# Moving the last pair's two GpSimd sums to VectorE in a spectral-mixing and SiLU kernel

## The chip, the cores and the metric

The kernel runs on one core of one Trainium2 chip. A core has five engines with separate instruction streams: TensorE (PE, matmuls, with its weight loads shown as PEld), VectorE (DVE), ScalarE (ACT), GpSimd (POOL) and SyncE (SP, which here only issues DMA). They wait for each other through semaphores. The metric is device time in microseconds (us), lower is better. The span that a profile shows is from the first to the last instruction of one execution; the time reported for that execution is a little longer.

## The reference

Two blocks follow each other. The first is a circular convolution over the sequence, by FFT; the second is a two-layer network with SiLU on every token.

```python
def _attn_ref(x, filt_r, filt_i):          # x: (8, 3008, 256)
    X = np.fft.rfft(x, axis=1)
    F = (filt_r + 1j * filt_i)[None, :, :]
    y = np.fft.irfft(X * F, n=x.shape[1], axis=1)
    return y.astype(np.float32)

def _moe_ref(x, w_in, w_out):              # x: (24064, 256), w_in: (256, 2048), w_out: (2048, 256)
    h = x @ w_in
    g = h * (1.0 / (1.0 + np.exp(-h)))
    return (g @ w_out).astype(np.float32)
```

## The kernel before

The transforms are done as small matrix products and spread over the kernel as hidden work; their pieces are put at fixed places of a timetable. The frame of the kernel is the second block. The tokens are cut into 48 pairs of token groups (256 or 240 tokens to a group); each pair goes through 8 steps, one for two blocks of 128 of the 2048 hidden channels. A step has two halves: `hidden(step)` makes the hidden values (seven products instead of eight, after Strassen, with the sums that this needs on VectorE and ScalarE, and SiLU on ScalarE), and `project(step)`, one step later, multiplies them with the second weight and accumulates seven products in four PSUM banks, `acc` 0 to 3. Both halves are generators, taken in turn, so that the order of the instructions on each engine is written out by hand. No scheduler changes it.

When the eighth step of a pair has been accumulated, the sums in PSUM become four output blocks. For all pairs but the last this is done by `drain` (from line 1093 on): ScalarE and VectorE copy the banks into a tile `s` of 8 slots in SBUF, GpSimd makes seven sums of slots, and SyncE issues two stores. The last pair has nothing behind it that could hide this, so it has its own function, `drain_last` (line 1107, called at line 1086 of `project`), which takes each half bank as soon as its last product is there. `(i, h)` names bank and half. The slots are filled in this order: copies on ScalarE for 0, 4 and 1 (line 1114), sums on VectorE, which read one operand from PSUM, for 2, 5, 3 and 6, and at last slot 1 from slots 3 and 1. Slot 4, the sum of slots 4, 1 and 5, needs two sums of slots that lie in SBUF. Slots 2, 6, 1 and 4 are the outputs; `store` (line 1143) sends each one with a DMA of its own, on SyncE's queue (2 and 6) or ScalarE's (4 and 1).

All sums go through the helper `combine`, so they carry line 989 on whichever engine they run. After the last instruction of the kernel body each engine runs a closing sequence (line 1517): it drains, SyncE waits for all outstanding stores, every engine reports to GpSimd by a semaphore, and GpSimd then releases the engines and clears the semaphores.

Of the kernel before, what the change touches and what calls it, by code (L numbers as in the profile page):

```python
# [49 lines left out]
ALU = mybir.AluOpType  # L50
# [197 lines left out]
def kernel(  # L248
# [9 lines left out]
    nc = tc.nc  # L258
# [726 lines left out]
    v, gp = nc.vector, nc.gpsimd  # L985
    ty, g_t, acc, unfinished = {}, {}, {}, []

    def combine(eng, out, in0, in1, op):
        eng.tensor_tensor(out=out, in0=in0, in1=in1, op=op)  # L989
# [74 lines left out]
    def project(step):  # L1064

        pair, jp = divmod(step, NJP)
        n, g = pairs[pair][3], g_t.pop(step)
        if jp == 0:
            acc[pair] = {}
        last = jp == NJP - 1  # L1070

        order = PROJECT
        if jp == 0 and step in joined:
            order = PROJECT[0:2] + PROJECT[3:5] + PROJECT[2:3] + PROJECT[5:]
        elif jp == 0:
            order = PROJECT[2:3] + PROJECT[0:2] + PROJECT[3:]
        elif step == n_steps - 1:
            order = PROJECT[0:4] + PROJECT[5:6] + PROJECT[4:5] + PROJECT[6:]
        for c, k, i, h in order:
            if i not in acc[pair]:  # L1080
                acc[pair][i] = accps.tile([128, 2, 256], FP32, name=f"acc_{pair}_{i}", tag=f"a{i}")

            nc.tensor.matmul(out=acc[pair][i][:, h, 0:n], lhsT=w_t[:, jp, c, 1], rhs=g[:, k, 0:n],  # L1083
                             start=(jp == 0 and h == 0), stop=last, skip_group_check=True)
            if last and pair == len(pairs) - 1:
                drain_last(pair, i, h, n, acc[pair])
            elif last and (h == 1 or i == 3):
                drain(pair, i)
            yield
# [17 lines left out]
    def drain_last(pair, i, h, n, sums):  # L1107

        if pair not in results:
            results[pair] = spool.tile([128, 8, CH], FP32, name=f"s_{pair}", tag="s")  # L1110
        s = results[pair]

        def copied(slot):
            nc.scalar.copy(out=s[:, slot, 0:n], in_=sums[i][:, h, 0:n])  # L1114

        def add(o, a, b=None, eng=v):
            combine(eng, s[:, o, 0:n], s[:, a, 0:n], sums[i][:, h, 0:n] if b is None else s[:, b, 0:n], ALU.add)
        if (i, h) == (0, 0):
            copied(0)
        elif (i, h) == (1, 0):  # L1120
            add(2, 0)
            store(pair, 2, nc.sync)
        elif (i, h) == (2, 0):
            copied(4)
        elif (i, h) == (0, 1):
            copied(1)
            add(4, 4, 1, gp)
        elif (i, h) == (2, 1):
            add(5, 0)
            add(4, 4, 5, gp)  # L1130
            store(pair, 4, nc.scalar)
        elif (i, h) == (1, 1):
            add(3, 5)
        else:
            add(6, 3)
            store(pair, 6, nc.sync)
            add(1, 3, 1)
            store(pair, 1, nc.scalar)

    def store(pair, slot, queue):  # L1140

        n = pairs[pair][3]
        queue.dma_start(out=out[pair, OUT_SLOTS.index(slot), :, 0:n], in_=results[pair][:, slot, 0:n])
# [378 lines left out]
```

## Time and profile before

| what | value |
|---|---|
| time, median of 3 runs | 2532.5 us (2532.28 to 2534.07) |
| time of the profiled execution | 2532.73 us |
| its span | 2530.6 us |
| granted TensorE clock | 0.996 |
| TensorE busy | 2505.6 us, 99% |
| VectorE, ScalarE, GpSimd busy | 69%, 43%, 17% |

On the page, a group's row gives the line, the engine and the operation, the output and the input tile, the partitions and elements, and the count; then the busy time and the mean length of one. A row of the timeline gives start and length in us from the start of the span, and in brackets the engine's idle time ahead of it with what released it. Rows of instructions that an engine's sequencer handles by itself (drains, semaphores, DMA issues) have a q behind the engine's name, and are not counted as busy.

### The profile page before, as it was taken

What the parts mean: (1) busy time and instruction counts of PE and PEld (TensorE: products, weight loads), DVE (VectorE), ACT (ScalarE), POOL (GpSimd) and SP (SyncE); (2) the same over time, 40 slices, a digit from 0 to 9 for tenths busy, and PEclk for the clock granted to TensorE, in tenths of its full rate; (3) what the DMA queues carried; (4) which work ended last, traced back from release to release, by engine and by line L of the source; (5) the groups of instructions that cost most, each with busy time, mean ns of one, the idle gap of its engine ahead of it and who ended that gap; (6) DMA issues with size and microseconds to landing.
All of it is one profiled execution on the core that took longest, in us unless ns stands there. A gap on an engine that the chain in (4) does not pass through costs nothing. (4 is left out here: it accounts for less than half of the span.)

```text
span 2530.6 us, 42130 instructions
## 1 busy us (share of the span) xinstructions
PE 2505.6 (99%) x16122; PEld 2142.8 (85%) x16122; DVE 1750.1 (69%) x3619; ACT 1096.7 (43%) x3012; POOL 435.1 (17%) x681
## 2 busy tenths in 40 slices
PE   8999999999999999999999999999999999999998
PEld 6788888888888888888888888888888888888987
DVE  7866777777767777677776767767677667655544
ACT  2544444444444444444444444444444444444443
POOL 3211211022111121211221112211121111101101
PEclk9999999999999999999999999999999999999999
DMA  9622142312332132420324203331142211200000
GB/s 289 169 67 88 63 109 58 80 51 63 76 85 63 41 80 59 95 73 20 92 58 108 60 25 77 85 72 43 28 107 58 55 43 34 63 21 9 17 9 17
DMA packets 145218, 171.49 MB, mean 68 GB/s; under 512 B 21396, under 2 KB 118772, under 8 KB 144132
## 3 DMA queue, kind: packets, MB, share of 16 engines
q1 hardware_dynamic: 119752, 117.85, 18.0%
q0 software_dynamic: 22272, 45.68, 7.0%
q10 hardware_dynamic: 2992, 5.28, 0.7%
q8 instruction: 126, 2.06, 0.4%
q14 instruction: 76, 0.62, 0.1%
HBM read 96.88 MB, written 81.26 MB: 70 GB/s over the span
## 5 line engine op out<-in xcount | busy, mean ns | idle before, releaser
L1083 PE MATMUL acc<-g,w_t 128*128 128x256 f32 (+1 forms) x5376 | 1509.5, 376 | 4.2 <-DVE q L818 3.7
L1083 PEld LDWEIGHTS acc<-g,w_t 128*128 128x128 f32 x5376 | 1017.1, 190 | 150.5 <-DVE q L818 19.0
L989 DVE TENSOR_TENSOR g<-pyz,abc 128x256 f32<-128x256 f32 (+1 forms) x1152 | 479.3, 416 | 501.7 <-ACT abc L1039 259.9
L989 DVE TENSOR_TENSOR g<-g 128x256 f32<-128x256 f32 (+3 forms) x1152 | 589.8, 512 | 196.9 <-ACT g L1022 183.7
L1018 PE MATMUL px<-ty,w_t 128*128 128x256 f32 (+1 forms) x2304 | 679.3, 377 | 1.5 <-ACT abc L1033 0.6
L1022 ACT ACTIVATE g<-g 128x256 f32<-128x256 f32 (+1 forms) x1152 | 472.9, 410 | 243.0 <-DVE g L989 243.0
L989 POOL TENSOR_TENSOR s<-s 128x256 f32<-128x256 f32 (+1 forms) x331 | 253.3, 783 | 1504.1 <-DVE s L1101 1099.8
L1018 PEld LDWEIGHTS px<-ty,w_t 128*128 128x128 f32 x2304 | 433.0, 190 | 65.3 <-ACT abc L1033 6.9
L1018 PE MATMUL pyz<-y,w_t 128*128 128x256 f32 (+1 forms) x1536 | 453.2, 377 | 0.8 <-DVE g L989 0.6
L1018 PEld LDWEIGHTS pyz<-y,w_t 128*128 128x128 f32 x1536 | 283.6, 190 | 46.4 <-DVE g L989 6.3
L1033 ACT COPY abc<-px 128x256 f32<-128x256 f32 (+1 forms) x384 | 141.4, 368 | 367.4 <-PE px L1018 367.4
L1039 ACT COPY abc<-px 128x256 f32<-128x256 f32 (+1 forms) x384 | 141.8, 369 | 312.9 <-PE px L1018 312.8
L1022 ACT ACTIVATE g<-px 128x256 f32<-128x256 f32 (+1 forms) x384 | 146.1, 381 | 302.0 <-PE px L1018 302.0
L1018 PE MATMUL px<-y,w_t 128*128 128x256 f32 (+1 forms) x768 | 228.0, 379 | 0.9 <-DVE y L775 0.9
L1018 PE MATMUL pyz<-ty,w_t 128*128 128x256 f32 (+1 forms) x768 | 226.0, 376 | 0.2 <-DVE g L989 0.2
L1018 PEld LDWEIGHTS px<-y,w_t 128*128 128x128 f32 x768 | 144.1, 190 | 26.1 <-ACT t L447 4.9
L1018 PEld LDWEIGHTS pyz<-ty,w_t 128*128 128x128 f32 x768 | 142.2, 190 | 21.4 <-DVE g L989 1.0
L1026 ACT COPY abc<-px 128x256 f32<-128x256 f32 (+1 forms) x384 | 135.5, 353 | 37.2 <-PE px L1018 37.2
L1101 ACT COPY s<-acc 128x512 f32<-128x512 f32 (+1 forms) x94 | 54.3, 578 | 47.5 <-issue 28.5
L646 POOL DMA_DIRECT2D d<-low x36 | 22.3, 618 | 288.9 <-DVE low L642 288.9
L818 DVE STREAM_TRANSPOSE q<-pd 128x512 f32<-128x512 f32 x84 | 57.2, 699 | 3.2 <-PE pd L797 3.2
L827 DVE TENSOR_TENSOR y<-q 128x384 f32<-128x384 f32 x112 | 56.1, 542 | 0.0
(159 smaller groups left out, 1367.5 us busy)
## 6 DMA issues: line engine op xcount, KB each, us to landing
t<-d SPq DMA_DIRECT2D x84, 256.0 KB
t<-d SPq DMA_DIRECT2D x224, 96.0 KB
out_dram<-s SPq DMA_DIRECT2D x64, 256.0 KB
d<-q POOLq DMA_DIRECT2D x48, 256.0 KB, 5.3
d<-low POOLq DMA_DIRECT2D x36, 256.0 KB, 4.2
xr<-in_x_dram SPq DMA_DIRECT2D x6, 1472.0 KB
out_dram<-s SPq DMA_DIRECT2D x30, 240.0 KB
x_all<-in_x_dram SPq DMA_DIRECT2D x72, 96.0 KB
```

Of the source, the lines that this page charges most:

```text
L646: nc.gpsimd.dma_start(out=d2[a0:a0 + 8, 16 * end:16 * end + 16], in_=part)
L818: nc.vector.transpose(out=t.rearrange("p (n a c) -> p n a c", n=8, a=2), in_=us["pd", k][r].rearrange("p a c -> p (a c)").rearrange("p (n ...
L827: nc.vector.tensor_tensor(out=dst[:, :, :, at:at + n], in0=even[:, :, :, 0:n], in1=odd[:, :, :, 0:n], op=op)
L989: eng.tensor_tensor(out=out, in0=in0, in1=in1, op=op)
L1018: nc.tensor.matmul(out=out, lhsT=w_t[:, jp, c, 0], rhs=rhs, start=start, stop=True, skip_group_check=True)
L1022: nc.scalar.activation(out=g[:, k, 0:n], in_=g[:, k, 0:n] if src is None else src, func=AFT.Silu)
L1026: nc.scalar.copy(out=sums[:, 0, 0:n], in_=xo)
L1033: nc.scalar.copy(out=sums[:, 1, 0:n], in_=xo)
L1039: nc.scalar.copy(out=sums[:, 2, 0:n], in_=xo)
L1083: nc.tensor.matmul(out=acc[pair][i][:, h, 0:n], lhsT=w_t[:, jp, c, 1], rhs=g[:, k, 0:n], start=(jp == 0 and h == 0), stop=last, skip_group ...
L1101: copy(out=s[:, 2 * i:2 * i + 2, 0:n], in_=acc[pair][i][:, :, 0:n])
```

## The change

For the last pair, slot 4's two sums move from GpSimd to VectorE. The first (slots 4 and 1) moves from the place of bank 0, half 1 to that of bank 2, half 1, behind VectorE's sum of slot 5. The second (slots 4 and 5) and slot 4's store move from there to the place of bank 1, half 1, behind VectorE's sum of slot 3. The store stays on ScalarE's queue. GpSimd's last sum is then the seventh one of `drain` for the pair before.

```diff
-        def add(o, a, b=None, eng=v):
-            combine(eng, s[:, o, 0:n], s[:, a, 0:n], sums[i][:, h, 0:n] if b is None else s[:, b, 0:n], ALU.add)
+        def add(o, a, b=None):
+            combine(v, s[:, o, 0:n], s[:, a, 0:n], sums[i][:, h, 0:n] if b is None else s[:, b, 0:n], ALU.add)
...
         elif (i, h) == (0, 1):
             copied(1)
-            add(4, 4, 1, gp)
         elif (i, h) == (2, 1):
             add(5, 0)
-            add(4, 4, 5, gp)
-            store(pair, 4, nc.scalar)
+            add(4, 4, 1)
         elif (i, h) == (1, 1):
             add(3, 5)
+            add(4, 4, 5)
+            store(pair, 4, nc.scalar)
         else:
             add(6, 3)
             store(pair, 6, nc.sync)
```

On each engine the order of all other instructions stays the same.

## The prediction

> **What bounds the kernel now.** I read the page first, then the chain of waits near the end, then the stretches of the last microseconds, and last the closing instructions one by one, since only the tail is edited.
>
> ```profile
> span 2530.6 us, 42130 instructions
> ...
> PE 2505.6 (99%) x16122; PEld 2142.8 (85%) x16122; DVE 1750.1 (69%) x3619; ACT 1096.7 (43%) x3012; POOL 435.1 (17%) x681
> ```
>
> TensorE is busy for 99% of the span. Nothing in the diff touches a matmul, so the first 2522 us stay as they are; both kernels issue the same instructions in the same order on TensorE, ScalarE and SyncE, and on VectorE and GpSimd they differ only behind the last matmuls. What can move is the stretch after TensorE. The chain of waits there, as start, length and work:
>
> ```profile
> 2522.49 0.69 PE acc L1083 x2
> 2523.17 0.02 issue
> 2523.20 0.42 DVE s L989
> ...
> 2523.71 0.40 DVE s L989
> 2524.11 0.32 DVEq L1517
> ```
>
> The chain stops at 2524.11 + 0.32 = 2524.43, but the span runs to 2530.6. The last 6.2 us are on no row of the chain. The busy time by stretch says the same:
>
> ```profile
> 2522.50:2524.20 1.70, 1.06 (x4) 0.66 (x4) 1.30 (x4) 0.00 (x0) 1.38 (x2) 1.00 0.21 72
> 2524.20:2530.60 6.40, 0.00 (x0) 0.00 (x0) 0.23 (x1) 0.00 (x0) 0.00 (x0) 0.63 0.17 59
> ```
>
> Columns: stretch, length, then PE, PEld, DVE, ACT, POOL busy (times), clock, DMA share, GB/s. In the last 6.4 us only the end of one VectorE operation and some DMA are left. So the closing sequence (line 1517, issued by the program's end) must hold the time. Its rows, from four windows: engine and operation, count, ns min/median/max, first and last start.
>
> ```profile
> L1517 PEldq DRAIN  x1: 1120/1120/1120, 2522.5 to 2522.5; - x1
> L1517 POOLq DRAIN  x1: 6534/6534/6534, 2523.3 to 2523.3; - x1
> L1517 DVEq DRAIN  x1: 699/699/699, 2523.8 to 2523.8; - x1
> ...
> L1517 SPq EVENT_SEMAPHORE  x2: 28/28/28, 2526.1 to 2526.4; - x2
> L1517 SPq DRAIN  x2: 7/7/7, 2526.5 to 2526.5; - x2
> ...
> L1517 POOLq EVENT_SEMAPHORE  x4: 17/17/17, 2529.9 to 2530.5; - x4
> L1517 POOLq DRAIN  x3: 46/102/6534, 2523.3 to 2530.3; - x3
> ```
>
> Each engine drains and then reports; SyncE first waits for the last stores (its last two such waits pass at 2526.1 and 2526.4) and reports at 2526.5. GpSimd's drain starts at 2523.3 and lasts 6.534 us, to 2523.3 + 6.53 = 2529.8. Only then does GpSimd take the reports (2529.9), and 0.7 us later the program is over. GpSimd's drain is the last to come, 2529.8 - 2526.5 = 3.3 us after SyncE. That drain, not TensorE and not the stores, sets the end.
>
> **Why the drain is so late.** GpSimd's operations in the last 50 us, as start, length, operation, count and the idle time before:
>
> ```profile
> 2479.77 5.70 POOL L989 TENSOR_TENSOR s<-s 128x256 f32<-128x256 f32 x7 [42.52 <-DVE s L1101]
> 2522.55 1.46 POOL L989 TENSOR_TENSOR s<-s 128x240 f32<-128x240 f32 x2 [37.08 <-ACT s L1114]
> ```
>
> The second row is the two sums that the change takes away. The drain is issued while the second of them begins (2523.3). That one ends at 2522.55 + 1.46 = 2524.01, so the drain ends 2529.8 - 2524.0 = 5.8 us after GpSimd's last work. VectorE's drain ends at 2523.8 + 0.70 = 2524.5, 0.1 after its last sum. The 5.8 us belong to GpSimd alone.
>
> **The change, part by part.** First: GpSimd loses two sums. Its last operation then ends at 2479.77 + 5.70 = 2485.47. The drain comes next in its stream with no wait ahead of it, so it is issued there; if it again takes 5.8 us behind the last sum, it ends near 2491.3, under TensorE's work, which covers it until 2522. It would need 35 us more to matter. The end then goes by whichever engine reports last, SyncE at 2526.5: a gain of 3.3 us.
>
> Second: VectorE gets two sums in a row of five. VectorE's closing sums before, one a row, then the ScalarE copy that the first new sum needs:
>
> ```profile
> 2522.04 0.40 DVE L989 TENSOR_TENSOR s<-s,acc 128x240 f32<-128x240 f32 x1
> 2522.51 0.40 DVE L989 TENSOR_TENSOR s<-s,acc 128x240 f32<-128x240 f32 x1
> 2523.20 0.41 DVE L989 TENSOR_TENSOR s<-s,acc 128x240 f32<-128x240 f32 x1 [0.29 <-PE acc L1083]
> 2523.71 0.40 DVE L989 TENSOR_TENSOR s<-s,acc 128x240 f32<-128x240 f32 x1
> 2524.03 0.40 DVE L989 TENSOR_TENSOR s<-s 128x240 f32<-128x240 f32 x1
> ...
> 2522.06 0.36 ACT L1114 COPY s<-acc 128x240 f32<-128x240 f32 x1 [0.79 <-PE acc L1083]
> ```
>
> They are slots 2, 5, 3, 6, 1. The last two stand 2524.03 - 2523.71 = 0.32 us apart although each lasts 0.40, so a sum that waits for nothing recent starts 0.32 us behind the one before. The first new sum (4 + 1) goes between slots 5 and 3: its inputs are copies, the last of which ended at 2522.42, so it starts at 2522.51 + 0.32 = 2522.83 and ends at 2523.23. Slot 3 waits for TensorE until 2523.20, and VectorE could take it from 2522.83 + 0.32 = 2523.15: no delay. The second new sum (4 + 5) follows at 2523.20 + 0.32 = 2523.52 and ends at 2523.92. Slot 6 stood at 2523.71 and can start only at 2523.52 + 0.32 = 2523.84: **0.13 us late**. Slot 1 follows at 2524.16 instead of 2524.03, 0.13 late as well.
>
> Bounds of this cost, from the nearest rows. It cannot be below nothing: no sum on the way to the last store gets an earlier input. Its upper end is two dependent sums back to back:
>
> ```profile
> 2515.80 0.84 DVE L989 TENSOR_TENSOR g<-g 128x240 f32<-128x240 f32 x2
> ```
>
> So 0 to 0.84 us; I take 0.13, as the row with the 0.32 spacing is from the very place.
>
> One rule speaks for more. The Trainium skill, "VectorE: DVE Perf Modes", section "The DRAIN you can't avoid", says in substance that the next VectorE operation doesn't start until the pipe of the one before is empty. By it the five sums would stand 0.40 apart: 4 + 1 until 2523.31, slot 3 from there, 4 + 5 until 2524.12, slots 6 and 1 until 2524.92, against 2524.43 before: +0.49. The overlap of the last two rows above disagrees, so I keep 0.13.
>
> Third: the stores. The issues before, and the share of the DMA engines in 40 slices from 2524.8 to 2526.8:
>
> ```profile
> 2524.04 0.36 ACTq L1143 DMA_DIRECT2D out_dram<-s  x1
> 2524.14 0.35 SPq L1143 DMA_DIRECT2D out_dram<-s  x1
> L1143 ACTq DMA_DIRECT2D out_dram<-s x2: 363/397/431, 2524.0 to 2524.5; - x2
> DMA  0037998999999999999999520000000000000000
> ```
>
> Slot 4's store on ScalarE's queue waited for GpSimd until 2524.01; now it waits for VectorE until 2523.92 and goes 0.09 us earlier. Slot 6's store on SyncE's queue and slot 1's behind slot 4's on ScalarE's go 0.13 later. Slot 4's issue ends at 2523.95 + 0.36 = 2524.31, before slot 1's sum does (2524.56), so it holds nothing up. The three stores fill the DMA engines almost without a gap until 2526.0, so the delay can pass on at most whole: SyncE's report goes from 2526.5 to 2526.6. No wait is added on TensorE: its last matmuls wait for VectorE's first sum (slot 2), which stands ahead of both new ones.
>
> **The sum.** -3.3 (drain gone from the end) + 0.13 (VectorE) = -3.2 us. Span 2530.6 - 3.2 = 2527.4. The profiled execution took 2532.73, 2.1 more than its span, so 2529.5; it lay 0.2 above the median of the runs (2532.5), so I predict **2529.4 us**, 0.12% below. A measurement of this kernel tells from no change only about 0.2% (5.1 us), so this counts as no change.
>
> **Rivals.** (a) The drain doesn't follow GpSimd's work but the end of the whole core, for example the last stores. It ended 3.4 us after SyncE's last store wait (2526.4), a distance no row explains. Then the change removes nothing and VectorE's delay of 0.13 to 0.84 is left: 2532.6 to 2533.3, slower than before from the first 0.1 us on. Against it: drains of the other engines end with their own work, and the drain at the program's start did too:
>
> ```profile
> L1506 POOLq DRAIN  x1: 174/174/174, 0.3 to 0.3; - x1
> L1506 POOL MEMSET const-uint8-127<- x1: 106/106/106, 0.3 to 0.3; 128x1 uint8 x1
> ```
>
> There the last memset is also at 0.3 and the drain lasts 0.17. It shows that a GpSimd drain can be short, but behind memsets and not behind sums. The same section of the Trainium skill calls the closing drains a constant of about 12 ns on all five engines, another kind than VectorE's; taken at its word GpSimd's own drain costs nothing, the 6.5 us would be a wait for something else, and (a) follows. The trace disagrees with the 12 ns (6,534 ns). Chance of (a) 0.08.
>
> (b) The 5.8 us fall on the first drain that GpSimd makes after standing idle, and come back in the closing sequence: GpSimd drains twice more behind the reports (46 and 102 ns above, right behind the long one), now after 35 us of waiting. At full price the end is 2527.4 + 5.8 = 2533.2, the time 2535.2; it is slower than before once more than 3.2 of the 5.8 us return. Against it: after 37.08 us of idling GpSimd's first sum lasted as long as the next (1.46 for both, with the gap). Chance 0.04.
>
> (c) The drain moves, but VectorE's sums stand serially or the stores collide, so that up to 0.84 is given back: 2530.0. It has the same sign and lies within my forecast.
>
> **How the numbers follow.** Forecast with (c): 0.86; (a) 0.08; (b) 0.04; unnamed 0.02. The forecast's bounds are 2529.2 (no VectorE delay) to 2530.0 (0.84 of it). The shown runs scatter from 0.2 below their median to 1.6 above, and the closing times are read to 0.1 us only, so I take 2528.6 to 2531.7. (a) and (b) lie outside it, 0.12 together. The bound of 0.2% is 2527.4 below and 2537.6 above: forecast, (a) and (b) all lie between. Same 0.92, faster 0.05 (a floor lower than the stores show, or run scatter), slower 0.03.
>
> **What would show it.** Right: GpSimd's long drain starts near 2485 and ends near 2491; GpSimd's first closing semaphore stands 0.1 us behind SyncE's report, near 2526.7; the span is 2527.4; five VectorE sums become seven, with slot 1's starting at 2524.16. Wrong by (a): a drain from 2485 to 2529 or later. Wrong by (b): one of the two later drains in microseconds. A last sum near 2524.5 instead of 2524.2 would show serial spacing.

## The result, and the profile after

The changed kernel takes 2528.59 us, the median of 22 runs (2526.49 to 2532.10); the kernel before, run beside it as often, takes 2532.44 us (2529.77 to 2538.01). The ratio is 0.9984, with a 95% interval of 0.9978 to 0.9989: a small gain, about 3.9 us. The prediction was 2529.4 us (range 2528.6 to 2531.7): the right direction and mechanism, the gain 0.8 us too small, so that the median lies just below the lower end of the range.

The profiled execution took 2527.65 us. The first line of the changed kernel's page:

```profile
span 2525.8 us, 42128 instructions
```

GpSimd's timeline in its last 50 us (start, length, operation, count, idle time before):

```profile
2478.39 5.71 POOL L989 TENSOR_TENSOR s<-s 128x256 f32<-128x256 f32 x7 [42.52 <-DVE s L1101]
```

And rows of its closing sequence (line 1517) from three windows, in the form used in the prediction:

```profile
L1517 POOLq DRAIN  x1: 7251/7251/7251, 2482.7 to 2482.7; - x1
...
L1517 SPq EVENT_SEMAPHORE  x10: 17/28/28, 2523.3 to 2524.9; - x10
...
L1517 POOLq EVENT_SEMAPHORE  x2: 17/17/17, 2525.1 to 2525.2; - x2
L1517 SPq DRAIN  x1: 7/7/7, 2525.1 to 2525.1; - x1
L1517 POOLq DRAIN  x1: 102/102/102, 2525.3 to 2525.3; - x1
```

GpSimd's long drain now starts at 2482.7 and ends at 2482.7 + 7.25 = 2489.9, again 5.8 us behind its last sum (2478.39 + 5.71 = 2484.10), under TensorE's work. At the end SyncE's last store wait passes at 2524.9, SyncE reports at 2525.1, and GpSimd takes the reports in the same tenth. The 3.3 us between the two are gone. VectorE's timeline of the changed kernel, its seven closing sums:

```profile
2520.65 0.87 DVE L989 TENSOR_TENSOR s<-s,acc 128x240 f32<-128x240 f32 x2
2521.44 0.40 DVE L989 TENSOR_TENSOR s<-s 128x240 f32<-128x240 f32 x1
2521.82 0.40 DVE L989 TENSOR_TENSOR s<-s,acc 128x240 f32<-128x240 f32 x1
2522.14 0.40 DVE L989 TENSOR_TENSOR s<-s 128x240 f32<-128x240 f32 x1
2522.46 0.40 DVE L989 TENSOR_TENSOR s<-s,acc 128x240 f32<-128x240 f32 x1
2522.77 0.40 DVE L989 TENSOR_TENSOR s<-s 128x240 f32<-128x240 f32 x1
```

Slots 2 and 5 share the first row; then come 4 + 1, 3, 4 + 5, 6 and 1. From slot 3 on they stand 0.32, 0.32 and 0.31 us apart though each lasts 0.40.

**Where the rest of the difference lies.** The two profiled executions differ by 5.1 us (2532.73 - 2527.65). Take two marks that both kernels have, GpSimd's sums of an early pair and of the last pair but one; the rows are from the kernel before:

```profile
198.27 5.56 POOL L989 TENSOR_TENSOR s<-s 128x256 f32<-128x256 f32 x7 [47.16 <-DVE s L1101]
```

and from the changed one:

```profile
196.83 5.57 POOL L989 TENSOR_TENSOR s<-s 128x256 f32<-128x256 f32 x7 [47.15 <-DVE s L1101]
```

The changed kernel is already 1.44 us ahead at 198 us (198.27 - 196.83), and still 1.38 ahead at 2480 (2479.77 - 2478.39). So 1.4 us arose before the first 200 us were over, where both kernels issue the same instructions, and nothing in the 2280 us between. The stretch from 50 to 100 us shows a likely source; its columns are PE, PEld, DVE, ACT, POOL busy (times), clock, DMA share, GB/s, first before, then changed:

```profile
50.00:100.00 50.00, 44.53 (x437) 33.86 (x437) 41.59 (x100) 26.31 (x56) 7.23 (x15) 0.83 0.77 227
```

```profile
50.00:100.00 50.00, 43.71 (x443) 32.10 (x442) 43.83 (x105) 26.79 (x57) 9.04 (x18) 0.90 0.76 224
```

There the granted clock was 0.83 and 0.90; over the whole first 156 us it was 0.95 and 0.96. In the twelve other profiles of this study TensorE passes the mark of 156 us between 3.7 us ahead of the kernel before and 2.9 us behind it (0.9 without the run with three drains below, which has two of them in that stretch), and keeps that distance to within 0.1 us until its end. The executions with the lower clock in the first 156 us tend to pass the mark later (0.93: 0.9 us behind; 1.00: 3.7 us ahead), but the clock isn't all of it: 0.98 stands beside 0.4 and beside 1.7 us ahead. So the 1.4 us are run scatter, and its cause is only in part shown.

That is why below the **tail** is compared: from the start of VectorE's sum of slot 3 to the end of the span. It was 2530.6 - 2523.20 = 7.4 us and is 2525.8 - 2521.82 = 4.0, a gain of 3.4. A last 0.3 us lies outside the span: the time around it fell from 2.1 (2532.73 - 2530.6) to 1.8 (2527.65 - 2525.84). The three parts, 1.4 + 3.4 + 0.3, make the 5.1.

### The profile page after: what moved, and what is told of

Its sections match the earlier page's. It is cut to its first block, busy times and chain, and to the rows that moved or that the text cites. A ratio compares the mean times of both kernels' runs of the same rounds, so it can differ in the third digit from the quotient of the medians.

```text
span 2525.8 us, 42128 instructions
## 1 busy us (share of the span) xinstructions
PE 2504.1 (99%) x16122; PEld 2140.9 (85%) x16122; DVE 1750.5 (69%) x3621; ACT 1095.2 (43%) x3012; POOL 433.7 (17%) x679
## 3 DMA queue, kind: packets, MB, share of 16 engines
q10 hardware_dynamic: 2992, 5.28, 0.7%
q8 instruction: 126, 2.06, 0.3%
```

## The experiments

All are profiled once on the chip; all but one start from the changed kernel. Tails and moments are read from the trace, counted in us from the start of VectorE's sum of slot 3 (written +/-).

**What starts the drain.** Three runs give GpSimd one operation back, whose result nobody reads.

A one-column copy, where the removed first sum stood:

```diff
             copied(1)
+            gp.tensor_copy(out=gate, in_=s[:, 1, 0:1])
```

> The changed kernel with one more GpSimd operation: a copy of one column of slot 1 into an unused tile, waiting for ScalarE's copy of slot 1, as the removed first sum did. Nothing reads it; VectorE keeps both sums. The tail is counted from the start of VectorE's slot 3 sum to the end of the span: 7.4 us before (2530.6 - 2523.20), 4.0 changed (2525.8 - 2521.82). Theory A (GpSimd's closing drain ends 5.8 us behind GpSimd's last operation of any kind): the copy starts some 0.65 us ahead of slot 3 and lasts a few tenths, the drain ends at +5.35, the tail is 6.1. Theory B (the 5.8 us come behind two-input sums only): 4.0. Theory C (the drain follows the end of the whole core): 7 or more.

A whole sum at that place:

```diff
             copied(1)
+            combine(gp, s[:, 7, 0:n], s[:, 4, 0:n], s[:, 1, 0:n], ALU.add)
```

> The changed kernel with one more GpSimd operation: the sum of slots 4 and 1 into the unused slot 7, 128x240, where the removed first sum stood. VectorE keeps both sums. It should end at about +0.04 us of slot 3's start. Theory A: drain until +5.85, tail 6.6. Theory B: the same. Theory C: no relation to the 0.04.

A memset:

```diff
             add(5, 0)
+            gp.memset(s[:, 0, 0:n], 0.0)
             add(4, 4, 1)
```

> The changed kernel with one more GpSimd operation: a memset of slot 0 (128x240) once VectorE's sum of slot 5 has read it, about 0.2 us ahead of slot 3. Theory A: it ends near 0.0 to +0.2, drain until +5.8 to +6.0, tail 6.5 to 6.8. Theory B, in the wider sense that only operations that read SBUF leave the 5.8 us (at the program's start the drain came 0.05 us behind a memset): tail 4.0.

| kernel | GpSimd's last operation ends | its drain ends | between | SyncE reports | tail |
|---|---|---|---|---|---|
| before | +0.82 | +6.62 | 5.81 | +3.34 | 7.4 |
| changed | -37.7 | -31.9 | 5.81 | +3.25 | 4.0 |
| late copy | -0.53 | +5.28 | 5.81 | +3.26 | 6.1 |
| late sum | -0.36 | +5.45 | 5.81 | +3.24 | 6.2 |
| late memset | +0.07 | +5.88 | 5.81 | +3.26 | 6.7 |

GpSimd's last operation in the run with the memset, from its timeline:

```profile
2523.30 0.30 POOL L1129 MEMSET s<- 128x240 f32 x1 [37.50 <-DVE s L989]
```

Its drain, from the rows of the closing sequence:

```profile
L1518 POOLq DRAIN  x1: 6126/6126/6126, 2523.3 to 2523.3; - x1
```

The memset ends at 2523.60 and the drain at 2523.3 + 6.13 = 2529.4: 5.8 us later, as behind a copy of one column and behind a sum. So the kind of operation doesn't matter (theory B falls), and the drain doesn't go by the stores' end (theory C, the prediction's rival (a)). The tail is the later of drain and report plus 0.8. In the run with the sum slot 3 itself starts 0.4 us late, because VectorE's 4 + 1 has to wait until GpSimd has read slot 4; counted from slot 2's sum the tail is 7.8, against 8.6 before, by the 0.8 us of the missing second sum.

**How early is early enough.** A copy released 3.9 us and one released 2.4 us ahead of slot 3's sum:

```diff
         silu(3, xo)
+        if step == n_steps - 1:
+            gp.tensor_copy(out=gate, in_=g[:, 3, 0:1])
```

> The changed kernel with a one-column GpSimd copy that waits for ScalarE's activation of slot 3 of the last step's hidden tile, which ends at 2517.88, 3.9 us ahead of VectorE's slot 3 sum. Theory A: the copy ends near -3.7, the drain near +2.1, SyncE's report (+3.25) stays the last and the tail stays 4.0. If GpSimd work anywhere in the last pair prolonged the end, the tail would be over 4.3.

```diff
             copied(0)
+            gp.tensor_copy(out=gate, in_=s[:, 0, 0:1])
```

> The changed kernel with a one-column GpSimd copy that waits for ScalarE's copy of slot 0, which ends at 2519.41, 2.4 us ahead of VectorE's slot 3 sum. Theory A: the copy ends near -2.2, the drain near +3.6, just behind SyncE's report at +3.25; the tail is 4.3 to 4.4. A drain with a shorter tail behind copies than behind sums leaves 4.0.

The first ends at -3.70, its drain at +2.11, and the tail is 4.0: free. The second ends at -1.92, its drain at +3.88, and the tail is 4.7, not the 4.3 to 4.4 expected, because this copy lasted 0.43 us where the others took 0.18 and 0.19; VectorE was adding from SBUF until just before it ended, which is the likely reason. Again 5.81 lie between, in both. So on this kernel GpSimd has to be done about 2.6 us (5.81 - 3.25) ahead of slot 3's sum, or it sets the end.

**GpSimd's part alone, undone.** Two GpSimd sums into an unused slot, with VectorE's two left in place:

```diff
             copied(1)
+            combine(gp, s[:, 7, 0:n], s[:, 0, 0:n], s[:, 1, 0:n], ALU.add)
...
             add(4, 4, 1)
+            combine(gp, s[:, 7, 0:n], s[:, 7, 0:n], s[:, 5, 0:n], ALU.add)
```

> The changed kernel with two more GpSimd sums into the unused slot 7, waiting for the same things as the two that the change removed; VectorE keeps its two. Only GpSimd's part of the change is undone. If that part alone makes the gain: drain until +6.6, tail 7.4, as before. If VectorE's two sums cost or gain something of their own, the tail differs from 7.4 by it (0.13 at most by the prediction).

The tail is 7.2, and counted from slot 2's sum 8.6 as before: all that the change gained in the tail is lost again, so it was GpSimd's part. But VectorE's sums look different while GpSimd adds at the same time. VectorE's timeline of this run, from 4 + 1 to 4 + 5:

```profile
2522.90 0.68 DVE L989 TENSOR_TENSOR s<-s 128x240 f32<-128x240 f32 x1
2523.50 0.39 DVE L989 TENSOR_TENSOR s<-s,acc 128x240 f32<-128x240 f32 x1
2523.82 0.58 DVE L989 TENSOR_TENSOR s<-s 128x240 f32<-128x240 f32 x1
```

GpSimd's timeline of the same run:

```profile
2522.62 1.50 POOL L989 TENSOR_TENSOR s<-s 128x240 f32<-128x240 f32 x2 [37.08 <-ACT s L1114]
```

The two sums with both operands in SBUF take 0.68 and 0.58 instead of 0.40; the one between, which reads one operand from PSUM, keeps its 0.39. The Trainium skill, "GPSIMD Engine Reference", section "Specifications", says that the two engines share SBUF interfaces and contend when a VectorE instruction has two SBUF inputs; this run agrees.

**VectorE and the stores.** More VectorE work, and another order of it:

```diff
             store(pair, 4, nc.scalar)
+            add(7, 0, 1)
         else:
             add(6, 3)
             store(pair, 6, nc.sync)
+            add(7, 0, 1)
             add(1, 3, 1)
```

> The changed kernel with two more VectorE sums (slots 0 and 1 into the unused slot 7): one ahead of the sum of slot 6, one ahead of the sum of slot 1. Slot 6's store is issued 0.32 us later and slot 1's 0.64 later. If the last issue sets the end: tail 4.0 + 0.64 = 4.6. If the stretch of three stores on the DMA engines sets it, started by slot 4's, part of the delay is absorbed: the data of slot 1's store starts some 0.85 us behind its issue, at +2.9, and is through at +3.2 instead of +2.75: tail 4.4 to 4.5. If VectorE's sums stand 0.40 apart: 0.8 later and tail 4.8.

```diff
         elif (i, h) == (2, 1):
-            add(5, 0)
             add(4, 4, 1)
+            add(5, 0)
         elif (i, h) == (1, 1):
-            add(3, 5)
             add(4, 4, 5)
             store(pair, 4, nc.scalar)
+            add(3, 5)
```

> The changed kernel with VectorE's order turned: 4 + 1 ahead of slot 5, and 4 + 5 ahead of slot 3. Slot 4's store is issued about 0.3 us earlier, the stores of slots 6 and 1 about 0.13 later. Since slot 3's sum itself moves by 0.3 here, the tail is counted from the start of the sum of slot 2, which stands ahead of all: 5.15 us in the changed kernel (2525.8 - 2520.65). If the stretch of stores started by slot 4's sets the end: 5.0 to 5.1. If the last issue sets it: 5.3.

| kernel | store of slot 4, 6, 1 issued | first to last data of these three | last issue to last data |
|---|---|---|---|
| before | +0.85, +0.94, +1.26 | +1.72 to +2.85: 1.13 | 1.59 |
| changed | +0.76, +1.06, +1.38 | +1.61 to +2.75: 1.14 | 1.37 |
| more sums | +0.76, +1.38, +2.15 | +1.61 to +3.47: 1.86 | 1.32 |
| slot 4 first | +0.11, +0.93, +1.25 | +0.97 to +2.61: 1.64 | 1.36 |

The tail with more sums is 4.8: the last store's issue came 0.77 us later than in the changed kernel and the end 0.8. It is more than the 0.64 expected since slot 1's sum started 0.44 us behind the added one, which reads the slot that it overwrites; the sums ahead of them still stand 0.32 us apart, so serial spacing isn't the reason. With slot 4 first, the tail from slot 2's sum is 5.4 against 5.2, by the 0.2 us (0.13 expected) that slot 1's store is issued later; that slot 4's went 0.3 us earlier gave nothing. So in the changed kernel the last issue sets the end, some 1.35 us ahead of the last data; in the kernel before, where the three were issued within 0.41 us, the last issue alone would give +2.61 (1.26 + 1.35) against the measured +2.85, so there the 1.13 us that they take together are the likely limit, though no run tests it. Both limits meet in the changed kernel, whose last data came at +2.75: 1.61 + 1.13 and 1.38 + 1.35 are 2.74 and 2.73. That fits VectorE's 0.13 us costing nothing: slot 1's store was issued 0.12 us later, but slot 4's began 0.1 us earlier, and SyncE's report came at +3.25 instead of +3.34.

**A DMA instead of a sum.** Slot 4's store on GpSimd's queue:

```diff
-            store(pair, 4, nc.scalar)
+            store(pair, 4, gp)
```

> The changed kernel with slot 4's store issued on GpSimd's queue instead of ScalarE's. No sum is moved. The issue comes at about +0.75 us of VectorE's slot 3 sum and on GpSimd lasts some 0.6 to 1.5 us. If a DMA issue leaves the same drain behind it as a sum: the drain ends at +1.4 to +2.3 plus 5.8, tail 8 to 9, 4 to 5 us over the changed kernel and slower than the kernel before. If issues leave no such drain: tail 4.0 to 5.

The issue in GpSimd's timeline of this run:

```profile
2522.78 0.60 POOL L1143 DMA_DIRECT2D out_dram<-s  x1 [38.74 <-DVE s L989]
```

The drain, from its closing rows:

```profile
L1517 POOLq DRAIN  x1: 6496/6496/6496, 2522.7 to 2522.7; - x1
```

The issue ends at 2523.38, the drain at 2529.2: 5.87 us behind it. The tail is 8.3, twice that of the changed kernel.

**What the drain works off.** In the runs so far 5.8 us is a constant behind whatever comes last. But at the program's start the drain was short. Three drains put in by hand, before GpSimd's first DMA, behind its first ones, and behind pair 20:

```diff
+    gp.drain()
+
     def idle(n, ps=None):
...
+    gp.drain()
+
     def tables():
...
             combine(gp, s[:, o, 0:n], s[:, a, 0:n], s[:, b, 0:n], ALU.add)
+        if pair == 20:
+            gp.drain()
```

> The changed kernel with three more drains in GpSimd's stream: the first behind the bias memsets, before GpSimd has issued any DMA; the second behind the first scaling of a table, when GpSimd has issued its share of the filter loads; the third behind the seven sums of pair 20, in the middle of the kernel. In seven runs the closing drain ended 5.81 us behind GpSimd's last operation, whatever that was, but the drain at the program's start ended 0.05 us behind a memset. Theory D (the 5.8 us come once GpSimd has issued DMAs): first drain under 0.3 us, second and third 5.8 us behind the operation ahead of them. Theory E (they belong to the closing sequence): all three short. Theory F (they come after long use of the engine only): only the third is long. The tail stays 4.0 in each.

The first ended 0.07 us behind the last memset, the second 6.3 us behind the scaling, the third 3.4 us behind the sums, and the closing one only 1.1. The second, with 16 DMA issues behind it, had data of them still in flight until 2 us before its end, so it says little, and it is left out of the fit below. None of D, E and F had 3.4 and 1.1. That gave theory G: a drain works off something that piles up between drains. Two runs test it, the first on the kernel before:

```diff
             combine(gp, s[:, o, 0:n], s[:, a, 0:n], s[:, b, 0:n], ALU.add)
+        if pair == len(pairs) - 2:
+            gp.drain()
```

> The kernel before, with its two GpSimd sums of the last pair, and one drain more in GpSimd's stream, behind the seven sums of the pair ahead of it, where GpSimd then stands idle for 37 us. Theory A as it stood (any late GpSimd operation puts the end 5.8 us behind itself): tail 7.4 as before, time as before. Theory G (a drain works off something that has piled up since GpSimd's previous drain, so the early one takes it away): the early drain lasts 5.8 us behind the last of the seven sums, the closing one ends 0.1 to 0.3 us behind the two sums, SyncE's report at +3.34 is the last again, and the tail is 4.1; the time falls by 3.3 us, to 0.9987 of before, with the sums where they were.

GpSimd's timeline of this run:

```profile
2476.22 5.71 POOL L989 TENSOR_TENSOR s<-s 128x256 f32<-128x256 f32 x7 [42.52 <-DVE s L1101]
2518.99 1.46 POOL L989 TENSOR_TENSOR s<-s 128x240 f32<-128x240 f32 x2 [37.06 <-ACT s L1116]
```

The rows of the added drain (line 1107) and of the closing one (line 1519):

```profile
L1107 POOLq DRAIN  x1: 7249/7249/7249, 2480.5 to 2480.5; - x1
...
L1519 POOLq DRAIN  x1: 797/797/797, 2519.7 to 2519.7; - x1
```

The two sums stand where they stood, and end at 2520.45; the closing drain ends at 2519.7 + 0.80 = 2520.5, 0.07 us behind them. The tail is 4.1. Timed, this kernel takes 2529.32 us (10 runs) against 2532.60 before (13 runs), ratio 0.9987 with an interval of 0.9978 to 0.9997. One instruction thus gets nearly all of the gain with VectorE untouched. The other run has drains at eight places:

```diff
             combine(gp, s[:, o, 0:n], s[:, a, 0:n], s[:, b, 0:n], ALU.add)
+        if pair in (8, 9, 20, 21, 32, 42, 44, 45):
+            gp.drain()
```

> The changed kernel with drains in GpSimd's stream behind the seven sums of pairs 8, 9, 20, 21, 32, 42, 44 and 45. Under theory G the length of each, counted from the end of the sum ahead of it, goes by what GpSimd did since the drain before: those of pairs 9 and 21 (one pair's work) a few tenths to 1 us, those of pairs 20 and 32 (11 pairs) 1 to 3.5 us, those of pairs 44 and 45 (sums only, since GpSimd's last DMA issue is behind them) near 0.1 if DMA issues are what piles up, or in proportion to the sums if those are. Under theory A all are 5.8 us. The tail is 4.0 in either case.

The rows of the drains behind pairs 20, 21, 42 and 44, each of which starts some 1.4 us ahead of the end of the last sum:

```profile
L1107 POOLq DRAIN  x1: 7989/7989/7989, 1171.8 to 1171.8; - x1
L1107 POOLq DRAIN  x1: 1842/1842/1842, 1223.1 to 1223.1; - x1
L1107 POOLq DRAIN  x1: 5601/5601/5601, 2289.1 to 2289.1; - x1
L1107 POOLq DRAIN  x1: 1452/1452/1452, 2385.7 to 2385.7; - x1
```

Counting GpSimd's sums and DMA issues between one drain and the next in all runs, beside the time from the last operation's end to the drain's end (the drains behind pairs 20 and 32 were expected at 1 to 3.5 us):

| drain | DMA issues | sums | us behind the last operation |
|---|---|---|---|
| eight drains: pairs 44, 45; closing | 0 | 14, 7, 7 | 0.08, 0.07, 0.07 |
| pairs 9, 21 | 4 | 7 | 0.41, 0.40 |
| pair 42 | 50 | 70 | 4.16 |
| pairs 20, 32 | 80 | 77 | 6.61, 6.61 |
| pair 8 | 94 | 83 | 7.77 |
| three drains: closing | 134 | 182 | 1.14 |
| three drains: pair 20 | 162 | 167 | 3.44 |
| before, changed: closing | 312 | 351, 349 | 5.81 |
| store on GpSimd's queue: closing | 313 | 349 | 5.87 |

The sums count for nothing: behind 14 sums and no DMA the drain ends 0.08 us later. What counts is the DMA issues since the last drain. Up to 94 of them it is 0.07 us plus 0.082 for each (80 x 0.082 + 0.07 = 6.63); for 134, 162, 312 and 313 it is as if 121, 121, 242 and 242 of them were taken off (70 x 0.082 + 0.07 = 5.81 for 312). That step of 121 is fitted to these four counts; what happens between 94 and 134, and why, isn't settled by these runs.

Two other readings fall by the same trace. It isn't the amount moved: the 94 issues up to pair 8 moved 12.1 MB in 5120 packets and the 80 up to pair 20 moved 11.6 MB in 5824 packets, while the time grows from 6.61 to 7.77 us; the four behind pair 9 moved 1.1 MB. Nor is it a wait for data: except in the last row, the data of GpSimd's last DMA was through over 12 us before the drain began.

## Why the prediction was right or wrong

- **The drain holds the end, not TensorE or the stores: right.** Rivals (a) and (b) are excluded: in ten kernels the closing drain follows GpSimd's own last operation by 5.81 us wherever that stands, and the two later drains stayed short (102 ns in the row above).
- **"If it again takes 5.8 us behind the last sum": right, and for a reason that the prediction didn't have.** The 5.8 us aren't a price of sums. They go with the 312 DMA issues that no drain had followed; the sums only set when the drain could begin, and with an earlier drain the closing one ends 0.07 us behind them.
- **VectorE's sums 0.32 apart, slot 6 and slot 1 0.13 late: right** (slot 6's start moved from +0.51 to +0.64). The rule of the Trainium skill weighed there, "VectorE: DVE Perf Modes", section "The DRAIN you can't avoid", would have had 0.40. But the same paragraph adds that a next operation which isn't held starts earlier, and the 0.32 fit that; the prediction didn't weigh it. The section's 12 ns for closing drains on all engines fit the other engines' second drains (7 to 19 ns in the profile before), not GpSimd's.
- **"So the delay can pass on at most whole: SyncE's report goes from 2526.5 to 2526.6": the step that was mis-sized.** I put +0.13 into the sum; it measured -0.09 (+3.25 against +3.34), as the three stores' time on the DMA engines began earlier. The tail gained 3.4 us, not 3.2. The lower bound of nothing was wrong too: no sum gets an earlier input, but slot 4's store does. This is 0.2 of the missing 0.8 us.
- **"2.1 more than its span": the other step that was mis-sized; taken as fixed, it fell to 1.8.** It isn't scatter: 22 runs of the changed kernel have 1.75 to 1.85, 13 of the kernel before 2.06 to 2.18. It is also 2.1 with two GpSimd sums given back, 1.8 or 1.9 with one late operation or none, and 1.9 to 2.1 with the two sums and an earlier drain. What it holds isn't shown, so why it fell stays open. This is 0.3 of the 0.8 us.
- **The sum itself was 0.1 high.** 2527.4 + 2.1 - 0.2 is 2529.3, not 2529.4, and the price of (b) by the same terms is 2535.1, not 2535.2. The rest of the 0.8 us, some 0.2, is within the scatter of the two medians.
- **The range was too narrow.** 3.4 + 0.3 is 3.7 us, the medians differ by 3.85. The lower end of 2528.6 came from three runs that scattered from 0.2 below to 1.6 above their median; 22 runs go from 2.7 below to 5.6 above. A likely part of its source, the low granted clock early in the kernel, stood in the profile before (0.83 from 50 to 100 us), and I didn't use it. That a measurement tells only about 0.2% from no change was shown by no run, and it was too modest: with 22 runs a side 0.16% is clear of no change, though inside that bound.

## What to carry to other kernels

When the chain of waits stops short of the span's end, list the closing drains and reports engine by engine; the last to report sets the time, and on GpSimd that can be long after its work. A GpSimd that has issued DMAs should either finish early enough before SyncE's report (5.8 us behind 312 issues here, 7.8 us behind 94), or drain once while it has nothing to do; keep late DMA issues off its queue. Where runs scatter by more than the effect, compare a stretch between two marks of the trace that the change leaves alone.

## What the runs showed of the hardware

- GpSimd's drain ended 0.07 us plus 0.082 us for each DMA that GpSimd had issued since its last drain behind GpSimd's last operation, up to 94 issues (0.41 us for 4, 7.77 for 94); for 134 to 313 it was as if 121 or 242 of them didn't count (1.14 for 134, 5.81 for 312). VectorE's drain ended 0.1 us behind its last sum, as the prediction's rows show.
- VectorE's sums of two SBUF operands slowed from 0.40 to 0.58 and 0.68 us beside a GpSimd sum, and a one-column GpSimd copy from 0.19 to 0.43 beside a VectorE sum; a VectorE sum with one PSUM operand kept 0.39.
- Between 156 us and TensorE's last product, thirteen other executions kept step with that of the kernel before to within 0.1 us over some 2365 us. The scatter between them, from 3.7 us ahead to 0.9 behind (2.9 in the run with two added drains early in the kernel), came earlier.
